# Linear attention and a routed expert layer on one core: the attention's matmuls in fewer array shapes, with a bank for the logits

## The chip, the cores and the metric

One core of a Trainium2 chip runs the whole program. The time is device time in microseconds (us) of one execution; the figure compared is the median of several runs. Lower is better. The engines: PE is TensorE (PEld its weight loads), DVE is VectorE, ACT is ScalarE, POOL is GpSimd, SP issues most DMAs.

## The reference

A gated linear attention over 4 batches and 8 heads, 768 positions, 48 channels, and then an expert layer in which every token goes to one of 8 experts with a capacity of 384 tokens:

```python
for t in range(S):
    state = alpha[:, :, t, :, None] * state + np.einsum('bhd,bhe->bhde', k[:, :, t], v[:, :, t])
    y[:, :, t] = np.einsum('bhd,bhde->bhe', q[:, :, t], state)
...
x = attn_out.transpose(0, 2, 1, 3).reshape(B * S, H * D)     # 3072 x 384
logits = x @ w_gate                                          # 3072 x 8
order = np.argsort(-logits.flatten())                        # best pairs first, each expert at most N // E tokens
...
out[mask] = np.maximum(x[mask] @ w1[e], 0.0) @ w2[e]         # for each expert e
```

## The kernel before

The attention is cut into chunks of C = 128 positions, 6 for each batch. A step `s` (24 in all) works on four chunks `u` of one pair of heads `p`; four steps with the same `g` make a group of 512 tokens. Channels lie on partitions, the two heads of a pair at 0 and at 64 (48 channels each, padded to 64). A step does this:

- DMA loads `al`, `rk`, `rq`, `rv` (alpha, k, q, v).
- VectorE scans alpha backwards into `te` (L349: the product of alpha from a position to the end of its chunk) and forwards into `tp` (L353). `zb`, two banks of PSUM, holds the additive term of the scans; its entries at the starts of chunks are set by a small copy (L364) and a reciprocal (L369). POOL multiplies: `kh` = k times `te`, `qh` = q times `tp` (L361; VectorE in step 0).
- `ends` (L357, VectorE) puts each chunk's whole decay, once for each head with zeros for the other (`hm` is a mask of ones and zeros), into `m`, one of six small buffers in `zb`.
- TensorE transposes `kh` (L378) and ScalarE copies it to `kn`. Scores `kh` x `qh` (L390), 64 rows by 128 columns of the array for each head; ScalarE copies them to `sm` and POOL masks them.
- State products `kn` x `rv` (L406, `st`), 48 columns for each head, outputs at partitions 0 and 64. VectorE (L420; ScalarE for a first chunk, L417) carries them from chunk to chunk into `ts`. `carried` (L426) multiplies the four states with `m` into `sb`, 128 columns wide, the off-diagonal blocks zero.
- The output `yb`: `inter` (L434, the carried product) multiplies `sb`, 128 columns, with `qh`; `intra` (L441, the masked product) adds `sm` x `rv`, 48 columns for each head. ScalarE copies it to `yt` (L444).
- TensorE turns `yt` into rows (L378 again), ScalarE copies them to `xg` (L454), and after four steps they are stored in `x_dram` (L458).
- Logits (L469): for the step two before, in the same operation as the state products and in the same bank, `yt` is the weight (128 columns) and 8 columns of `wg` are the data, a part for each pair `p`. After the fourth, VectorE sums the four parts (L479) into `L`.

The order on each engine is written out beforehand by a list scheduler, `Plan.order`: each operation has a cost, buffers (`Kind`, with a given number of tiles), operations that it must follow, a rank, and on TensorE a `mode`, the array's shape. Among those that can start within `SLACK` of the first it takes the highest rank, with a bonus of `SAME` for the mode that stands; a change of mode is costed at `SWITCH`. Each engine then runs its list in that order and waits where data is not there. The framework keeps two engines apart that touch the same PSUM bank. `choice(b)` puts the first part of the routing (the best expert of each token, the first comparison and counts) for 12, 8 and 4 token blocks into the same list, ranked low.

After the attention, the tokens of an expert are found by a search (L604 comparisons on VectorE, L651 counts on TensorE, L660), and gathered; then come two matrix products for each expert (L868, L888).

Of the kernel before, what the change touches and what calls it, by code (L numbers as in the profile page):

```python
# [8 lines left out]
F32 = mybir.dt.float32  # L9
# [9 lines left out]
AF = mybir.ActivationFunctionType  # L19
OP = mybir.AluOpType  # L20
# [18 lines left out]
class Plan:  # L39
# [10 lines left out]
    def add(self, eng, cost, fn, r=(), w=(), lat=None, port=False, mode=None):  # L50
        n = len(self.ops)
        before, bufs = set(), []
        for x in r:
            if x in self.writer:
                before.add(self.writer[x])
            self.readers.setdefault(x, []).append(n)
        for x in w:
            before.update(self.readers.pop(x, ()))
            if x in self.writer:
                before.add(self.writer[x])  # L60
            self.writer[x] = n
# [83 lines left out]


HOP = {"PE": 0.3, "DVE": 0.15, "ACT": 0.2, "POOL": 0.2, "SP": 2.2}
SLACK, SAME, SWITCH = 0.1, 3.0, 0.15


@with_exitstack
def gla_moe_kernel(ctx, tc, q, k, v, alpha, w_gate, w1, w2, out):
    nc = tc.nc
    C = 128
    NC = 6
    H = 8
    HP = H // 2
# [4 lines left out]
    D = Dm // H  # L162
    E = w_gate.shape[1]
# [3 lines left out]
    consts = ctx.enter_context(tc.tile_pool(name="consts", bufs=1))  # L167
# [4 lines left out]
    ident = consts.tile([128, 128], F32)  # L172
    make_identity(nc, ident)
    L = consts.tile([128, NU, E], F32)
    wg = consts.tile([128, HP, 32], F32)

    T = 128
    BITS = (7, 7, 6, 6, 6)
# [88 lines left out]
    NS = NG * HP  # L267
    X = mybir.AxisListType.X
# [6 lines left out]
    def ring(n, shape, name, ordered=True):  # L275
        return Kind([ap_.tile(shape, F32, name=f"{name}{i}") for i in range(n)], ordered)
# [3 lines left out]
    TE, TP = ring(3, [128, 4 * C], "te"), ring(2, [128, 4 * C], "tp")  # L280
# [17 lines left out]

    nc.vector.memset(zb, 0.0)
    for h in range(2):  # L300
        nc.vector.memset(hm[64 * h:64 * h + 64, h:h + 1], 1.0)
    nc.vector.memset(ST.tiles[0], 0.0)
    nc.gpsimd.memset(wg, 0.0)
    for t in SB.tiles + TS:
        nc.gpsimd.memset(t, 0.0)
# [27 lines left out]
    def step(s):  # L333
        g, p = divmod(s, HP)
        al, rk, rq, rv = load(s)
        te, tp, kh, qh, kn, sm, m, sb, yt = (pl.buf(x) for x in (TE, TP, KH, QH, KN, SM, MR, SB, YT))
        xt, sc, yb, st = (pl.buf(x) for x in (XT, SC, YB, ST))
        parts = 2 if s < 2 else 1
        w = 4 * C // parts
        for j in range(parts):  # L340
            lo, hi = j * w, (j + 1) * w
            us = slice(lo // C, hi // C)
            n = us.stop - us.start

            def each_u(b):
                return [(b, u) for u in range(us.start, us.stop)]

            def scan_e(lo=lo, hi=hi):
                nc.vector.tensor_tensor_scan(te.t[:, lo:hi][:, ::-1], al.t[:, lo + 1:hi + 1][:, ::-1],  # L349
                                             zb[:, lo + 1:hi + 1][:, ::-1], 1.0, op0=OP.mult, op1=OP.add)  # L350

            def scan_p(lo=lo, hi=hi):
                nc.vector.tensor_tensor_scan(tp.t[:, lo:hi], al.t[:, lo:hi], zb[:, lo:hi], 1.0,  # L353
                                             op0=OP.mult, op1=OP.add)

            def ends(us=us, lo=lo, hi=hi, n=n):
                nc.vector.tensor_tensor(m.t[:, us], te.t[:, lo:hi:C][:, :, None].to_broadcast([128, n, 2]),  # L357
                                        hm[:, None, :].to_broadcast([128, n, 2]), op=OP.mult)

            def mul(eng, out_, x, f, us=us, lo=lo, hi=hi):  # L360
                eng.tensor_tensor(out_.t[:, us].rearrange("p u c -> p (u c)"), x.t[:, lo:hi], f.t[:, lo:hi], op=OP.mult)  # L361

            if j == 0:
                add(V, 0.1, lambda: nc.vector.tensor_copy(zb[:, C:4 * C + 1:C], al.t[:, 4 * C + 1:4 * C + 5]),  # L364
                    r=[al], w=["Z"])
            add(V, 0.06 + 0.285 * n, scan_e, r=[al], w=each_u(te) + ["Z"])
            ek, ck, en = (V, 0.08 + 0.15 * n, nc.vector) if s == 0 else (G_, 0.06 + 0.28 * n, nc.gpsimd)
            add(ek, ck, lambda f=mul: f(en, kh, rk, te), r=each_u(te) + [rk], w=each_u(kh), port=True)
            add(V, 0.17, lambda lo=lo, hi=hi: nc.vector.reciprocal(zb[:, lo:hi:C], te.t[:, lo:hi:C]),  # L369
                r=each_u(te), w=["Z"])  # L370
            add(V, 0.06 + 0.285 * n, scan_p, r=[al, "Z"], w=each_u(tp))
# [24 lines left out]

        us_st = [u for u in every if chunk(s, u) < NC - 1]

        back = ys.pop(s - 2, None)

        def state():
            if back:
                logit(st, *back)
            for u in us_st:
                for h in range(2):
                    nc.tensor.matmul(st.t[64 * h:64 * h + D, u, :D], kn.t[:, u, 64 * h:64 * h + D], rv.t[:, u, h],  # L406
                                     start=True, stop=True)
# [16 lines left out]
        def carried():  # L424
            t = ts[:, 4:0:-1] if g % 2 else ts[:, 0:4]
            nc.vector.tensor_tensor(sb.t[:, :, :, :D], t[:, :, None, :].to_broadcast([128, 4, 2, D]),  # L426
                                    m.t[:, :, :, None].to_broadcast([128, 4, 2, D]), op=OP.mult)
        add(V, 0.5, carried, r=[("T", p), m], w=[sb])

        us_y = [u for u in every if chunk(s, u)]  # L430

        def inter():
            for u in us_y:
                nc.tensor.matmul(yb.t[:, u], sb.t[:, u].rearrange("p h d -> p (h d)"), qh.t[:, u],  # L434
                                 start=(u == us_y[0]), stop=False, skip_group_check=True)
# [8 lines left out]
        add(A_, 0.6, lambda: nc.scalar.activation(yt.t, yb.t, AF.Copy), r=[yb], w=[yt])  # L444

        if p == 0:
            grp["xg"] = pl.buf(XG)
        xg = grp["xg"]
        ys[s] = s, yt

        def rows():
            x3 = pl.buf(XT)
# [7 lines left out]
                    r=[(xg, i) for i in range(HP)])  # L460
        return rows

    grp, ys = {}, {}
    wg_ = [("wg", 0), ("wg", 1)]

    def logit(st, s, yt):
        g, p = divmod(s, HP)
        for u in range(4):
            nc.tensor.matmul(st.t[:, p, D + E * u:D + E * u + E], yt.t[:, u], wg[:, p, :E], start=True, stop=True)  # L469

    def logit_reads(back):
        return [back[1]] + wg_ if back else []

    def gather_logits(st, back):
        if not back:
            return
        g, p = divmod(back[0], HP)
        if p == HP - 1:
            add(V, 0.25, lambda: nc.vector.tensor_reduce(  # L479
                L[:, 4 * g:4 * g + 4].rearrange("p u e -> p (u e)"),  # L480
                st.t[:, :, D:D + 4 * E].rearrange("p b x -> p x b"), axis=X, op=OP.add), r=[st], w=[("L", g)])

    def last_logits(s):
        st, back = pl.buf(ST), ys.pop(s)
        add(P_, 0.6, lambda: logit(st, *back), r=logit_reads(back), w=[st], mode=128)
        gather_logits(st, back)
    consts_ = ['init%d' % i for i in range(40)]
    BATCHES = ((0, 3), (3, 5), (5, 6))

# [489 lines left out]
```

## Time and profile before

| | |
|---|---|
| median of 3 runs | 453.09 us (452.11 to 453.66) |
| the profiled execution | 454.3 us, span 452.6 us |
| attention, first VectorE work to the last logits | 8.1 to 147.1 us of the span |
| routing of the first expert | about 147 to 174 us |
| experts | about 174 us to the end |
| mean granted clock of TensorE | 0.934 |

The profile has a page (busy time of each engine; the span in 40 slices, a digit for each) and views of the trace: groups of instructions, what waited for what, the chain that ended last, the order of time, stretches. Times are from the span's start. A row such as `72.08 1.16 PE L434 MATMUL y<-qh,sb 128*128 128x128 f32 x8` reads: start, length until the last of them ends, engine, line, operation, output<-inputs, rows*columns of the array, the data streamed, and how many records; an fp32 matmul leaves two records, a transpose one. Lengths of neighbouring matmul groups overlap, since matmuls are pipelined; from start to start is the better measure.

### The profile page before, as it was taken

Reading aid. Unit: us, or ns where it says so; the run is one execution under the profiler, and the core shown is the slowest. Engines: PE = TensorE matmul, PEld = TensorE weight load, DVE = VectorE, ACT = ScalarE, POOL = GpSimd, SP = SyncE. Lnnn points to the kernel's source line nnn. Section 1 sums busy time; section 2 is a strip of 40 time slices with the busy share of each in tenths; the row PEclk is TensorE's granted clock in tenths of the full one; section 3 lists DMA queues with packets and bytes.
Section 4 is the critical chain, followed back from the end, with each engine's and each line's share of the span. In section 5 each row is a group of like instructions: output and inputs, shape, how many; then the busy total and the mean of one; then the engine's idle time right before and its main releaser. Section 6 shows DMA issues by size and latency. Waiting matters only on the chain.

```text
span 452.6 us, 10133 instructions
## 1 busy us (share of the span) xinstructions
PE 411.9 (91%) x3976; PEld 371.5 (82%) x3976; DVE 276.4 (61%) x816; ACT 213.0 (47%) x353; POOL 187.2 (41%) x196
## 2 busy tenths in 40 slices
PE   3899999999999338998999999999999999999992
PEld 1688888888888235788898998888988999999992
DVE  6998777799772576267686685865866641312110
ACT  1445544554542006336728456373645666575311
POOL 6686666666750005104415255064064062440202
PEclk8899999999999655589999999989999999999997
DMA  8967886753010127979999999999795999996101
GB/s 288 375 193 244 283 275 187 246 177 106 19 71 2 70 92 169 228 133 318 190 246 262 215 292 269 224 282 206 215 271 137 269 272 313 252 238 121 54 0 52
DMA packets 44080, 88.85 MB, mean 196 GB/s; under 512 B 3840, under 2 KB 18176, under 8 KB 44032
## 3 DMA queue, kind: packets, MB, share of 16 engines
q0 software_dynamic: 11776, 34.61, 36.0%
q1 hardware_dynamic: 32256, 53.60, 35.6%
q8 instruction: 31, 0.51, 0.4%
q14 instruction: 17, 0.14, 0.1%
HBM read 53.59 MB, written 9.44 MB: 139 GB/s over the span
## 4 chain that ended last, share of the span: by engine, by line
PE 67%; DVE 12%; issue 9%; DMA 6%; ACT 2%; POOL 2%; POOLq 0%; SPq 0%; DVEq 0%; ACTq 0%
PE h L868 17%; PE y L888 16%; PE rt L651 6%; PE st L469 5%; PE s L390 5%; PE y L441 4%; PE y L434 4%; PE xt L378 4%; DMA w1r<-in_moe_w_dram 3%; DVE cmp L604 2%; PE st L406 2%; DMA w1lo<-w1r 2%; DVE tp L353 1%; DVE te L349 1%; PE xt L852 1%
## 5 line engine op out<-in xcount | busy, mean ns | idle before, releaser
L873 DVE SCALAR_TENSOR_TENSOR hl<-h,hh 128x384 fp32r<-128x384 f32 x64 | 35.4, 554 | 63.9 <-ACT hh L872 61.8
L872 ACT ACTIVATE hh<-h 128x384 fp32r<-128x384 f32 x64 | 31.0, 486 | 79.0 <-PE h L868 69.2
L888 PE MATMUL y<-w2hi,hh 128*128 128x384 f32 x192 | 66.9, 348 | 0.8 <-ACT hh L872 0.8
L888 PE MATMUL y<-w2hi,hl 128*128 128x384 f32 x192 | 66.2, 346 | 0.0
L888 PE MATMUL y<-w2lo,hh 128*128 128x384 f32 x192 | 66.0, 344 | 0.0
L899 POOL DMA_INDIRECT out_dram<-yt,idx x24 | 29.0, 1208 | 58.6 <-ACT yt L892 53.7
L799 POOL DMA_INDIRECT xr<-x_dram,idx x24 | 30.6, 1275 | 51.9 <-DVE val L730 30.2
L868 PE MATMUL h<-xh,w1lo 128*128 128x384 f32 x192 | 48.8, 355 | 1.0 <-DMA w1lo<-w1r 1.0
L827 ACT ACTIVATE w1hi<-w1r 128x768 fp32r<-128x768 f32 x32 | 26.9, 839 | 48.1 <-DVE val L720 21.9
L868 PE MATMUL h<-xl,w1hi 128*128 128x384 f32 x192 | 48.5, 354 | 0.0
L868 PE MATMUL h<-xh,w1hi 128*128 128x384 f32 x192 | 48.3, 356 | 0.0
L832 POOL DMA_DIRECT2D w1lo<-w1r x16 | 22.0, 1378 | 52.8 <-ACT w1lo L828 30.4
L361 POOL TENSOR_TENSOR kh<-rk,te 128x512 f32<-128x512 f32 (+1 forms) x24 | 29.4, 1225 | 34.8 <-DVE z L369 27.3
L651 PEld LDWEIGHTS <-cmp 128*128 128x128 bf16 x816 | 30.5, 118 | 15.3 <-DVE cmp L604 12.4
L651 PE MATMUL rt<-o,cmp 128*128 128x8 bf16 x816 | 33.1, 175 | 8.6 <-DVE cmp L604 8.6
L888 PEld LDWEIGHTS y<-w2hi,hh 128*128 128x128 f32 x192 | 36.6, 190 | 1.9 <-ACT hh L872 1.1
L868 PEld LDWEIGHTS h<-xh,w1lo 128*128 128x128 f32 x192 | 35.6, 197 | 2.0 <-DMA w1lo<-w1r 1.6
L868 PEld LDWEIGHTS h<-xl,w1hi 128*128 128x128 f32 x192 | 35.4, 197 | 2.0 <-issue 1.8
L888 PEld LDWEIGHTS y<-w2lo,hh 128*128 128x128 f32 x192 | 36.5, 190 | 0.3 <-DMA w2lo<-w2r 0.3
L888 PEld LDWEIGHTS y<-w2hi,hl 128*128 128x128 f32 x192 | 36.5, 190 | 0.1
L868 PEld LDWEIGHTS h<-xh,w1hi 128*128 128x128 f32 x192 | 35.7, 198 | 0.8 <-ACT xh L855 0.7
L832 POOL DMA_DIRECT2D w2lo<-w2r x16 | 15.7, 980 | 47.3 <-ACT w2lo L828 46.7
(164 smaller groups left out, 847.0 us busy)
## 6 DMA issues: line engine op xcount, KB each, us to landing
w1r<-in_moe_w_dram SPq DMA_DIRECT2D x16, 768.0 KB, 7.5
w2r<-in_moe_w_dram SPq DMA_DIRECT2D x16, 768.0 KB, 7.9
w1lo<-w1r POOLq DMA_DIRECT2D x16, 768.0 KB
w2lo<-w2r POOLq DMA_DIRECT2D x16, 768.0 KB
al<-in_alpha_dram SPq DMA_DIRECT2D x24, 260.0 KB, 4.2
rk<-in_k_dram SPq DMA_DIRECT2D x24, 256.0 KB, 3.6
rq<-in_q_dram SPq DMA_DIRECT2D x24, 256.0 KB, 4.2
rv<-in_v_dram SPq DMA_DIRECT2D x24, 192.0 KB, 2.5
```

What stands on the lines that cost most here:

```text
L361: eng.tensor_tensor(out_.t[:, us].rearrange("p u c -> p (u c)"), x.t[:, lo:hi], f.t[:, lo:hi], op=OP.mult)
L390: nc.tensor.matmul(sc.t[:, h, u], kh.t[hs, u], qh.t[hs, u], start=True, stop=True)
L469: nc.tensor.matmul(st.t[:, p, D + E * u:D + E * u + E], yt.t[:, u], wg[:, p, :E], start=True, stop=True)
L651: nc.tensor.matmul(cnt, cmp[:, j // U, :, j % U], o[:, j], start=(j == 0), stop=(j == NU - 1))
L799: last_gather[0] = nc.gpsimd.indirect_dma_start(out=XR[i][:, b], out_offset=None, in_=x_dram, in_offset=bass.IndirectOffsetOnAxis(ap=IDX[i ...
L827: nc.scalar.activation(hi[ix_], raw_[ix_], AF.Copy)
L832: nc.gpsimd.dma_start(lo.bitcast(F32), raw_, accum_op=OP.add, max_dma_last_dim=8192)
L868: nc.tensor.matmul(o, a[:, d], x[:, d], start=(n == 0), stop=(n == 3 * DB - 1))
L872: nc.scalar.activation(hh, o, AF.Relu)
L873: nc.vector.scalar_tensor_tensor(hl, o, 0.0, hh, op0=OP.max, op1=OP.subtract)
L888: F2[i, q] = nc.tensor.matmul(Y[b], a[:, bs], w, start=(q == 0 and n == 0), stop=(q == FB - 1 and n == 2))
L899: st_ = nc.gpsimd.indirect_dma_start(out=out, out_offset=bass.IndirectOffsetOnAxis(ap=IDX[i][:, b:b + 1], axis=0), in_=yt, in_offset=None)
```

## The change

- The carried product runs as two matmuls of 64 columns for each chunk, one for each head, with outputs at partitions 0 and 64. It is given the planner's mode 48, that of the masked product and the states.
- The logits are computed in the step itself, as soon as `yt` is there: `wg`, now 64 columns wide with zeros behind the 8, is the weight, and `yt` streams, 128 columns; two chunks for each half of the array. All four steps of a group add up in a bank `LG` of their own. After the fourth, ScalarE copies them (`lt`), TensorE turns them into rows and VectorE copies the 8 columns into `L`. The reduction L479 is gone, and so are the logits after the last step.
- `zb` shrinks to one bank, which makes room for `LG`. The mask `hm` and the factors `m8` move into unused columns of the bank of the states, `ST`; a step's factors are held with its states.
- Since `zb` no longer has a column behind the last position, the last column of `te` is copied by ScalarE, and the scan starts one position earlier from a value read from `al`.
- `choice(b)` enters the list two steps earlier. The planner's constants change.

```diff
-SLACK, SAME, SWITCH = 0.1, 3.0, 0.15
+SLACK, SAME, SWITCH = 0.02, 6.0, 0.17
...
-    wg = consts.tile([128, HP, 32], F32)
+    wg = consts.tile([128, HP, 64], F32)
...
-    SC, YB, ST = (Kind([bank(n, [128, x, 4, C] if x > 1 else [128, 4, C])])
-                  for n, x in (("s", 2), ("y", 1), ("st", 1)))
-    zb = bank("z", [128, 8 * C])
-    MR = Kind([zb[:, 5 * C + 8 * i:5 * C + 8 * i + 8].rearrange("p (u c) -> p u c", c=2) for i in range(6)])
-    hm = zb[:, 6 * C:6 * C + 2]
+    SC, YB, ST, LG = (Kind([bank(n, [128, x, 4, C] if x > 1 else [128, 4, C])])
+                      for n, x in (("s", 2), ("y", 1), ("st", 1), ("lg", 1)))
+    zb = bank("z", [128, 4 * C])
+    hm = ST.tiles[0][:, 0, D:D + 2]
+    LT = ring(2, [128, 2, C], "lt")
...
             def scan_e(lo=lo, hi=hi):
-                nc.vector.tensor_tensor_scan(te.t[:, lo:hi][:, ::-1], al.t[:, lo + 1:hi + 1][:, ::-1],
-                                             zb[:, lo + 1:hi + 1][:, ::-1], 1.0, op0=OP.mult, op1=OP.add)
+                top = min(hi, 4 * C - 1)
+                nc.vector.tensor_tensor_scan(te.t[:, lo:top][:, ::-1], al.t[:, lo + 1:top + 1][:, ::-1],
+                                             zb[:, lo + 1:top + 1][:, ::-1],
+                                             al.t[:, 4 * C + 4:4 * C + 5] if hi == 4 * C else 1.0,
+                                             op0=OP.mult, op1=OP.add)
...
-            def ends(us=us, lo=lo, hi=hi, n=n):
-                nc.vector.tensor_tensor(m.t[:, us], te.t[:, lo:hi:C][:, :, None].to_broadcast([128, n, 2]),
-                                        hm[:, None, :].to_broadcast([128, n, 2]), op=OP.mult)
...
+            add(A_, 0.2, lambda: nc.scalar.activation(te.t[:, 4 * C - 1:], al.t[:, 4 * C + 4:4 * C + 5], AF.Copy),
+                r=[al], w=[(te, 3, "last")])
...
-            add(V, 0.16, ends, r=each_u(te), w=[m])
...
-        back = ys.pop(s - 2, None)
-
         def state():
-            if back:
-                logit(st, *back)
             for u in us_st:
...
-        add(P_, 0.045 * len(us_st) + (0.6 if back else 0.0), state, r=[kn, rv] + logit_reads(back), w=[st], mode=48)
-        gather_logits(st, back)
+        add(P_, 0.045 * len(us_st), state, r=[kn, rv], w=[st], mode=48)
+        m8 = ST.tiles[0][:, 1, D:D + 8].rearrange("p (u c) -> p u c", c=2)
+        add(V, 0.17, lambda: nc.vector.tensor_tensor(
+            m8, te.t[:, 0::C][:, :, None].to_broadcast([128, 4, 2]), hm[:, None, :].to_broadcast([128, 4, 2]),
+            op=OP.mult), r=[(te, u) for u in every], w=[(st, "m")])
...
-                                    m.t[:, :, :, None].to_broadcast([128, 4, 2, D]), op=OP.mult)
-        add(V, 0.5, carried, r=[("T", p), m], w=[sb])
+                                    m8[:, :, :, None].to_broadcast([128, 4, 2, D]), op=OP.mult)
+        add(V, 0.55, carried, r=[("T", p), (st, "m")], w=[sb])
...
             for u in us_y:
-                nc.tensor.matmul(yb.t[:, u], sb.t[:, u].rearrange("p h d -> p (h d)"), qh.t[:, u],
-                                 start=(u == us_y[0]), stop=False, skip_group_check=True)
-        add(P_, 0.225 * len(us_y), inter, r=[sb] + [(qh, u) for u in every], w=[yb], mode=128)
+                for h in range(2):
+                    nc.tensor.matmul(yb.t[64 * h:64 * h + 64, u], sb.t[:, u, h], qh.t[:, u],
+                                     start=(u == us_y[0]), stop=False, skip_group_check=True)
+        add(P_, 0.225 * len(us_y), inter, r=[sb] + [(qh, u) for u in every], w=[yb], mode=48)
...
+        def logit():
+            for b in range(2):
+                for h in range(2):
+                    nc.tensor.matmul(lg.t[64 * h:64 * h + 64, b], wg[:, p], yt.t[:, 2 * b + h], start=(p == 0 and b == 0),
+                                     stop=(p == HP - 1 and b == 1), skip_group_check=True)
+        add(P_, 0.43, logit, r=[yt, ("wg", 0), ("wg", 1)], w=[lg], mode=48)
+        if p == HP - 1:
+            lt, x2 = pl.buf(LT), pl.buf(XT)
+
+            def turn_logits():
+                for b in range(2):
+                    nc.tensor.transpose(x2.t[:, b], lt.t[:, b], ident)
+            add(A_, 0.4, lambda: nc.scalar.activation(lt.t, lg.t[:, :2], AF.Copy), r=[lg], w=[lt])
+            add(P_, 0.22, turn_logits, r=[lt], w=[x2], mode=128)
+            add(V, 0.2, lambda: nc.vector.tensor_copy(
+                L[:, 4 * g:4 * g + 4].rearrange("p (b h) e -> p b h e", h=2),
+                x2.t[:, :2].rearrange("p b (h e) -> p b h e", h=2)[:, :, :, :E]), r=[x2], w=[("L", g)])
...
-    def logit(st, s, yt):
-        g, p = divmod(s, HP)
-        for u in range(4):
-            nc.tensor.matmul(st.t[:, p, D + E * u:D + E * u + E], yt.t[:, u], wg[:, p, :E], start=True, stop=True)
...
-            add(V, 0.25, lambda: nc.vector.tensor_reduce(
-                L[:, 4 * g:4 * g + 4].rearrange("p u e -> p (u e)"),
-                st.t[:, :, D:D + 4 * E].rearrange("p b x -> p x b"), axis=X, op=OP.add), r=[st], w=[("L", g)])
...
-        if s == NS - 1:
-            last_logits(s - 1)
-            last_logits(s)
         for b, (_, y) in enumerate(BATCHES):
-            if y * HP + 1 == (s if s < NS - 1 else s + 2):
+            if y * HP - 1 == s:
```

More of the change, by code (lines that the diff above doesn't have):

```diff
@@ L292, in gla_moe_kernel @@
     XT = Kind([bank("xt", [128, 4, C], psx) for _ in range(2)], ordered=False)
-    SC, YB, ST = (Kind([bank(n, [128, x, 4, C] if x > 1 else [128, 4, C])])
-                  for n, x in (("s", 2), ("y", 1), ("st", 1)))
-    zb = bank("z", [128, 8 * C])
-    MR = Kind([zb[:, 5 * C + 8 * i:5 * C + 8 * i + 8].rearrange("p (u c) -> p u c", c=2) for i in range(6)])
-    hm = zb[:, 6 * C:6 * C + 2]
+    SC, YB, ST, LG = (Kind([bank(n, [128, x, 4, C] if x > 1 else [128, 4, C])])
[3 more added lines that the diff above has]
+    LT = ring(2, [128, 2, C], "lt")
     nc.vector.memset(zb, 0.0)
+    nc.vector.memset(LG.tiles[0], 0.0)
+    nc.vector.memset(ST.tiles[0], 0.0)
     for h in range(2):
         nc.vector.memset(hm[64 * h:64 * h + 64, h:h + 1], 1.0)
-    nc.vector.memset(ST.tiles[0], 0.0)
     nc.gpsimd.memset(wg, 0.0)
@@ L335, in step @@
         al, rk, rq, rv = load(s)
-        te, tp, kh, qh, kn, sm, m, sb, yt = (pl.buf(x) for x in (TE, TP, KH, QH, KN, SM, MR, SB, YT))
+        te, tp, kh, qh, kn, sm, sb, yt = (pl.buf(x) for x in (TE, TP, KH, QH, KN, SM, SB, YT))
         xt, sc, yb, st = (pl.buf(x) for x in (XT, SC, YB, ST))
@@ L363, in step @@
             if j == 0:
-                add(V, 0.1, lambda: nc.vector.tensor_copy(zb[:, C:4 * C + 1:C], al.t[:, 4 * C + 1:4 * C + 5]),
+                add(V, 0.165, lambda: nc.vector.tensor_copy(zb[:, C:4 * C:C], al.t[:, 4 * C + 1:4 * C + 4]),
                     r=[al], w=["Z"])
-            add(V, 0.06 + 0.285 * n, scan_e, r=[al], w=each_u(te) + ["Z"])
+                add(A_, 0.2, lambda: nc.scalar.activation(te.t[:, 4 * C - 1:], al.t[:, 4 * C + 4:4 * C + 5], AF.Copy),
+                    r=[al], w=[(te, 3, "last")])
+            add(V, 0.08 + 0.285 * n, scan_e, r=[al], w=each_u(te) + ["Z"])
             ek, ck, en = (V, 0.08 + 0.15 * n, nc.vector) if s == 0 else (G_, 0.06 + 0.28 * n, nc.gpsimd)
-            add(ek, ck, lambda f=mul: f(en, kh, rk, te), r=each_u(te) + [rk], w=each_u(kh), port=True)
+            add(ek, ck, lambda f=mul: f(en, kh, rk, te), r=each_u(te) + [rk, (te, 3, "last")], w=each_u(kh), port=True)
             add(V, 0.17, lambda lo=lo, hi=hi: nc.vector.reciprocal(zb[:, lo:hi:C], te.t[:, lo:hi:C]),
                 r=each_u(te), w=["Z"])
-            add(V, 0.06 + 0.285 * n, scan_p, r=[al, "Z"], w=each_u(tp))
+            add(V, 0.08 + 0.285 * n, scan_p, r=[al, "Z"], w=each_u(tp))
             add(ek, ck, lambda f=mul: f(en, qh, rq, tp), r=each_u(tp) + [rq], w=each_u(qh), port=True)
-            add(V, 0.16, ends, r=each_u(te), w=[m])
         def turn(dst, src):
@@ L446, in step @@
         if p == 0:
-            grp["xg"] = pl.buf(XG)
-        xg = grp["xg"]
-        ys[s] = s, yt
+            grp["xg"], grp["lg"] = pl.buf(XG), pl.buf(LG)
+        xg, lg = grp["xg"], grp["lg"]
+        def logit():
[14 more added lines that the diff above has]
+                x2.t[:, :2].rearrange("p b (h e) -> p b h e", h=2)[:, :, :, :E]), r=[x2], w=[("L", g)])
         def rows():
@@ L461, in step @@
         return rows
-    grp, ys = {}, {}
-    wg_ = [("wg", 0), ("wg", 1)]
-    def logit(st, s, yt):
-        g, p = divmod(s, HP)
-        for u in range(4):
[L469 to L479, printed above, removed]
-                L[:, 4 * g:4 * g + 4].rearrange("p u e -> p (u e)"),
-                st.t[:, :, D:D + 4 * E].rearrange("p b x -> p x b"), axis=X, op=OP.add), r=[st], w=[("L", g)])
[L483 to L486, printed above, removed]
+    grp = {}
     consts_ = ['init%d' % i for i in range(40)]
```

## The prediction

> **What bounds the kernel now.** I read the page first (span, engine shares, clock), then the table of stretches, then the order of time of one step in the middle of the attention, then the waits, and last the handover to the routing. The page:
>
> ```profile
> span 452.6 us, 10133 instructions
> PE 411.9 (91%) x3976; PEld 371.5 (82%) x3976; DVE 276.4 (61%) x816; ACT 213.0 (47%) x353; POOL 187.2 (41%) x196
> PEclk8899999999999655589999999989999999999997
> ```
>
> The profiled execution took 454.3 us for this span of 452.6 us; the median of the runs is 453.09 us (452.11 to 453.66), 1.2 us less. I add up against 454.3 and take the 1.2 us off at the end. The clock row is low in slices 14 to 18, the routing after the attention; in the attention TensorE has its full clock. The stretch from VectorE's first work to the end of its last product with the carried states:
>
> ```profile
> 8.00:142.30 134.30, 128.66 (x1604) 112.93 (x1604) 108.85 (x252) 63.80 (x109) 83.84 (x73) 0.98 0.59 193
> ```
>
> TensorE is busy in 128.7 of 134.3 us (after the length stand the busy us of TensorE's matmuls and weight loads, VectorE, ScalarE and GpSimd, called POOL, then clock and DMA). Nothing but that stretch is edited, and the rest starts after it, so a microsecond taken from it is a microsecond of the whole. One step of 24, on TensorE, in order of time (start, length, group):
>
> ```profile
> 65.32 1.16 PE L390 MATMUL s<-qh,kh 64*128 64x128 f32 x16
> 66.41 1.16 PE L434 MATMUL y<-qh,sb 128*128 128x128 f32 x8
> 67.50 1.08 PE L441 MATMUL y<-sm,rv 128*48 128x128 f32 x16
> 68.51 1.06 PE L469 MATMUL st<-wg,yt 128*128 128x8 f32 x8
> 69.50 0.47 PE L406 MATMUL st<-rv,kn 128*48 128x48 f32 x12
> 69.90 0.66 PE L378 MATMUL xt<-ident,kh 128*128 128x128 f32 x4
> 70.39 0.60 PE L378 MATMUL xt<-ident,yt 128*128 128x128 f32 x4
> 70.92 1.16 PE L390 MATMUL s<-qh,kh 64*128 64x128 f32 x16
> ```
>
> From start to start: scores 1.09, carried product (L434) 1.09, masked product (L441) 1.01, logits (L469) 0.99, states (L406) 0.40, the two transposes 1.02; together 5.60 us, with no idle time. An fp32 matmul is two records. The masked product has 16 records where the carried one has 8 in hardly more time: its two heads, 48 columns each in the two halves of the array, run side by side. The four middle groups take 69.90 - 66.41 = 3.49 us and alternate between 128 and 48 columns.
>
> **What a record and a change of shape cost.** From the chain, where lengths run from start to start:
>
> ```profile
> 44.72 0.86 PE y L434 x6
> 80.78 0.49 PE st L406 x16
> 105.02 0.59 PE xt L378 x4
> ```
>
> Three carried calls take 0.86 and four 1.09, so one call is 0.23 and the rest, about 0.18, is the change of shape into and out of the group. Four transposes take 0.59 and eight 1.02: 0.108 a record, 0.15 for the change. If a pair of records of the masked product takes 0.108 too, its 8 pairs are 0.86 and the change is 0.15. States: 16 records 0.49, 12 records 0.40, so a pair is about 0.045 and the change 0.13. Once the planner put states and masked product, both of 48 columns, side by side:
>
> ```profile
> 140.29 0.47 PE L406 MATMUL st<-rv,kn 128*48 128x48 f32 x12
> 140.59 1.04 PE L441 MATMUL y<-sm,rv 128*48 128x128 f32 x16
> 141.57 0.43 PE L527 MATMUL xt<-o,cmp 128*128 128x8 bf16 x8
> ```
>
> The two take 1.28 us here against 0.40 + 1.01 = 1.41: one change less is worth 0.13 us.
>
> **The change part by part.**
>
> *Carried product as pairs of 64 columns, in one shape with its neighbours.* Four calls become eight in four pairs: 8 pairs of records at 0.108 are 0.86, as 4 x 0.23 = 0.91 before. The pairing itself gains almost nothing; what goes is the 0.18 of changing shape. No row has 64 columns. The nearest are these (weight loads of 48 and 128 columns, mean ns after the comma) with the paired rows of L441:
>
> ```profile
> L441 PEld LDWEIGHTS y<-sm,rv 128*48 128x48 f32 x384 | 19.8, 123 | 2.8 <-issue 0.3 <-POOL kh L361 0.2
> L434 PEld LDWEIGHTS y<-qh,sb 128*128 128x128 f32 x160 | 19.7, 191 | 3.7 <-DVE sb L426 0.8 <-ACT yt L444 0.5
> L417 ACT ACTIVATE ts<-st 128x48 f32<-128x48 f32 x16 | 3.4, 210 | 14.5 <-DVE ts L420 6.6 <-PE st L406 3.1 <-PE xt L378 2.7
> ```
>
> 68 ns more for 80 more columns is 0.85 ns a column, so a load of 64 columns takes 14 ns longer than one of 48, and about 54 ns of the array's time. A pair of records lasts 108 ns, so I take the load as hidden, as that of 48 columns is. Bounds: nothing, or the whole 54 ns in each pair of records (a rival below).
>
> *Logits the other way round.* Before: four calls with 128 columns of weights and 8 columns of data, 0.99 us with its changes of shape. After: wg's 64 columns are the weights and yt streams; four calls in two pairs, 4 pairs of records, 0.43 us.
>
> *Sum of the four groups*, where they stand together as one block: 0.86 + 0.86 + 0.43 + 0.27 (6 pairs of states) + 0.15 for one change = 2.57 instead of 3.49. With three carried calls 0.86 + 1.01 + 0.99 + 0.41 = 3.27 becomes 0.65 + 0.86 + 0.43 + 0.27 + 0.15 = 2.36. Either way 0.9 us a step. For how many steps? The first two are paced by others:
>
> ```profile
> 20.52 1.28 POOL qh L361
> 21.84 1.16 PE s L390 x16
> ```
>
> Only from step 2 on, at 21.84 us, is the chain on TensorE. 22 steps x 0.9 = 19.8 us off.
>
> *Logits back into rows, six times.* A ScalarE copy of 256 columns, two transposes and a VectorE copy replace a VectorE reduction. TensorE pays 2 x 0.108 = 0.22 if they stand beside other transposes, 0.37 alone: 1.3 to 2.2, I take 1.8 us on. ScalarE (64 of 134 us busy) and VectorE (a copy for a reduction) have it covered by other steps' work, except the last, below.
>
> *te's last column from ScalarE.* 26 one-column activations, at most the 0.21 us of the 48-column row: 5.5 us on ScalarE, hidden by its 70 idle us. They stand ahead of POOL's kh, which waits for them; queued behind one sm copy of about 1 us they would cost POOL that, and POOL has 50 us idle. I take nothing; without that cover it is 0.2 us for each of 24 steps, 5 us. The scan now reads its start value from memory: no row shows it. Between 0 and 0.1 us each (the 48-column ts update, which reads a factor so, is 0.1 us over a small copy), I take 0, at the most 2.4 us of VectorE.
>
> *Factors beside the states.* The 26 small products become 24, on the same engine, for the same 0.17 us. They now write the bank that TensorE's states use, so states of the next step wait until the carried product's operand sb has been made. Behind that wait stand, in TensorE's queue, the logits and transposes. The wait is covered: see VectorE's step.
>
> ```profile
> 65.31 0.55 DVE L426 TENSOR_TENSOR sb<-ts,z 128x384 f32<-128x384 f32 x1
> 65.98 1.21 DVE L349 TENSOR_TENSOR_SCAN te<-al,z 128x512 f32<-128x512 f32 x1
> 67.22 0.19 DVE L369 RECIPROCAL z<-te 128x4 f32<-128x4 f32 x1
> 67.52 1.22 DVE L353 TENSOR_TENSOR_SCAN tp<-al,z 128x512 f32<-128x512 f32 x1
> 68.77 0.17 DVE L364 COPY z<-al 128x4 f32<-128x4 f32 x1
> 68.97 0.17 DVE L357 TENSOR_TENSOR z<-te,z 128x8 f32<-128x8 f32 x1
> 70.02 0.86 DVE L420 SCALAR_TENSOR_TENSOR ts<-ts,te,st 128x48 f32<-128x48 f32 x3 [0.88 <-PE st L406]
> 70.92 0.55 DVE L426 TENSOR_TENSOR sb<-ts,z 128x384 f32<-128x384 f32 x1
> ```
>
> sb is made at 65.86 and the next states come at 69.50: 3.6 us of cover, 2.7 after the step has shrunk.
>
> *VectorE, the engine that is late next.* Its step of 5.61 us has 0.88 us of waiting, so 4.7 us of work and gaps, and TensorE's new step is 4.7. Over the stretch:
>
> ```profile
> DVE ts L420 <- PE st L406: 14.7, 13, 2.5
> DVE ts L420 <- ACT ts L417: 3.0, 7, 1.4
> ```
>
> With 0.8 more for the reduction these are 18.5 us of waits in 134.3: VectorE needs 115.8 us without any, TensorE now 134.3 - 19.8 + 1.8 = 116.3. Two engines so evenly loaded, with rings of two to four buffers between, will not both run without a gap. Bounds for what that costs: 0 (all waits vanish) to 6 (a third of them stays); I take 2.5, nearer to none because the planner can let routing work of low rank, which now becomes ready two steps earlier, slide into the end, where VectorE waits anyway.
>
> *The planner's constants* (a change of shape priced at 0.17, 6 us of preference for the same shape) let the four groups stand together; they have no price beyond the order.
>
> *The end.*
>
> ```profile
> 145.39 0.60 ACT L444 ACTIVATE yt<-y 128x512 f32<-128x512 f32 x1 [3.11 <-PE y L441]
> 146.04 0.97 PEld L469 LDWEIGHTS st<-wg,yt 128*128 128x128 f32 x8 [0.35 <-ACT yt L444]
> 146.95 0.64 PE L378 MATMUL xt<-ident,yt 128*128 128x128 f32 x4
> 147.14 0.29 DVE L479 TENSOR_REDUCE L<-st 128x32 f32<-128x128 f32 x1 [4.80 <-PE st L469]
> 148.14 0.38 SPq L458 DMA_DIRECT2D x_dram<-xg  x1
> 149.93 0.17 PE L658 MATMUL rt<-g,one 128*128 128x8 bf16 x1 [0.33 <-DVE g L535]
> 151.80 0.17 DVE L660 TENSOR_REDUCE k<-rt 128x1 f32<-128x8 f32 x1 [1.92 <-DMA x_dram<-xg]
> ```
>
> The search (k, 151.80) waits for the store of the last rows, not for the logits, which were through at 150.1. The logits' new way (copy under 0.5, transposes about 0.4, three handovers) is some 1 us longer and fits into these 1.7 us; if it did not, it would cost the excess. The store's way gets shorter, since the logits ahead of the last transposes take 0.5 instead of 0.9: 0.4 us off.
>
> **Sum:** -19.8 + 1.8 + 2.5 - 0.4 = -15.9, so 438.4 for an execution like the profiled one and 437.2 us against the median. With 0 to 6 us for the gaps it is 434 to 441.
>
> **The rivals.**
>
> *VectorE becomes the bound.* For it: 115.8 against 116.3 us. Against it: routing work can slide. With a third of its waits left (6.0) and 2.4 us for the scans: -19.8 + 1.8 + 8.4 - 0.4 = -10.0, 443.1 us.
>
> *48 and 64 columns are different shapes,* and changing between them costs the 0.13. Three borders a step: 22 x 0.39 = 8.6 us back, 445.8 us. Nothing in the trace speaks for or against. The Trainium skill, page TensorEngine Tiling (Array Packing), section Tiling Modes, lists tiles of 128, 64 and 32 columns, by which 48 and 64 would be one mode; no run here shows it.
>
> *The weight loads of a pair are exposed:* 54 ns in each of 2 x 3.33 + 4 = 10.7 pairs of records, 0.58 us a step, 12.7 us back: 449.9 us. Against it: a pair of L441 fits the 0.108 us of a transpose's record, with nothing over. The Trainium skill, page TensorE: Matmul & The Clock Gate, section Part 3: Packing small matmuls — row/col tiling, says that weight loads overlap running matmuls only where the row group differs, and in these pairs it is the same. By that rule this rival would be the forecast; the trace of the 48-column pairs disagrees.
>
> *The other side: the states wait for sb.* Place: L406 in TensorE's queue, behind VectorE's sb. If VectorE, now without slack, does a whole preparation (1.21 + 0.19 + 1.22 + 0.17 + 0.17 = 2.96) and a routing comparison of about 1 us before ts and sb, the 2.7 us of cover are exceeded by 1.2 us a step. It decides from 0.9 us a step on, where the gain is gone; at 1.2 it is 22 x 0.3 + 1.4 = 8 us more, 461 us. Against it: ts is made ahead of the next preparation in the rows above.
>
> **How the numbers follow.** Forecast 0.60, VectorE bound 0.20, shape borders 0.06, exposed loads 0.04, the wait for sb 0.10 (0.07 of it slower, 0.03 near no change). A difference under 0.3% (1.4 us) can't be told from none here. Faster 0.90, same 0.03, slower 0.07. The range goes from 434.0 (no gaps at all and the transposes at their cheapest are -18.9, so 434.2) to 446.5, past the shape borders; left out are the last two rivals and a little at the low end, under 0.2.
>
> **What would show it.** L434 with 16 records in about 0.87 us (half the starts coinciding), L469 with 8 in 0.43, no pause between the four groups, 4.7 us from scores to scores; VectorE's wait for the states below 6 us in the attention; the last store's issue near 132 us. Wrong it would be if L434's records came one after the other, if a gap of about 0.1 us stood between the 64- and 48-column groups, or if TensorE waited at L406 or L434 for VectorE by more than 0.3 us a step.

## The result and the profile after

The changed kernel takes 441.01 us (median of 3 runs, 440.52 to 441.85) against 453.09: ratio 0.9739, 95% interval 0.9703 to 0.9775, about 12 us less. Six further runs on another chip, beside eleven of the kernel before, gave 442.62 us and a ratio of 0.9793 (0.9748 to 0.9839), about 9 us less. Some executions of a kernel are slow, over 1.5% above its fastest; ratios leave them out, while a time with its range in brackets is the median of all. The profiled execution took 440.5 us for a span of 438.8 us. The experts' part, which the change leaves alone, took from 269 to 283 us in the profiled executions of this study, with 11 to 38 us of it at half clock; below I therefore compare stretches of the attention and not only whole times.

The page, as shown of the kernel before:

```profile
span 438.8 us, 10527 instructions
PE 398.1 (91%) x4148; PEld 359.3 (82%) x4148; DVE 276.2 (63%) x815; ACT 216.8 (49%) x383; POOL 185.0 (42%) x196
PEclk9999999999998565999998999969999999999997
```

A step on TensorE in which the planner made the full block (start, length, group; L454 is now the logits, L435 the carried product, L442 the masked product, L403 the states):

```profile
62.27 0.66 PE L454 MATMUL lg<-yt,wg 128*64 128x128 f32 x8
62.76 1.04 PE L435 MATMUL y<-qh,sb 128*64 128x128 f32 x16
63.63 1.04 PE L442 MATMUL y<-sm,rv 128*48 128x128 f32 x16
64.50 0.44 PE L403 MATMUL st<-rv,kn 128*48 128x48 f32 x12
64.87 0.66 PE L379 MATMUL xt<-ident,yt 128*128 128x128 f32 x4
65.36 0.60 PE L379 MATMUL xt<-ident,kh 128*128 128x128 f32 x4
65.89 0.66 PE L454 MATMUL lg<-yt,wg 128*64 128x128 f32 x8
66.48 1.16 PE L391 MATMUL s<-qh,kh 64*128 64x128 f32 x16
```

From 62.27 to 64.87 the four groups take 2.60 us; 3.49 before. The logits take 0.49, the carried product 0.87 and the masked one 0.87. Between 64 and 48 columns (62.76 to 63.63 to 64.50) there is no extra time. The next logits (65.89) stand alone between transposes and scores and take 0.59: they bring a change of shape of their own.

The places in the span, before and after, each read from the order of time:

| us of the span | before | after |
|---|---|---|
| first scan | 8.28 | 8.92 |
| scores of step 2 | 21.84 | 24.06 |
| scores of step 23 | 136.78 | 125.15 |
| search begins (k) | 151.80 | 140.34 |
| from step 2 to step 23 | 114.94 | 101.09 |
| from step 2 to the search | 129.96 | 116.28 |

So 13.7 us are won from step 2 on and 2.2 lost before it. The remaining 2.3 of the 13.8 us between the two profiled spans lie behind the search, within the scatter of the experts' part.

The waits of VectorE from its first work to the end of the attention:

```profile
DVE ts L420 <- ACT ts L417: 3.8, 7, 0.9
DVE ts L420 <- PE st L403: 2.9, 3, 1.3
DVE st L407 <- ACT ts L417: 0.6, 1, 0.6
```

They were 18.5 us and are 7.6 (with 0.3 for the copy of the logits). TensorE waited for sb, the feared place, 0.5 us in all, and at the states not at all. It stays the bound: from 24 to 125 us it is busy in 99.5 of 101.0 us, in the kernel before in 114.5 of 114.9 us from 21.8 to 136.7.

The start: the carried and the masked product of step 0 on TensorE, the same of step 1, and VectorE clearing the bank of y.

```profile
17.87 1.55 PE L435 MATMUL y<-qh,sb 128*64 128x128 f32 x12 [0.35 <-DVE sb L426]
19.21 1.73 PE L442 MATMUL y<-sm,rv 128*48 128x128 f32 x16
25.16 0.88 PE L435 MATMUL y<-qh,sb 128*64 128x128 f32 x12
25.86 1.04 PE L442 MATMUL y<-sm,rv 128*48 128x128 f32 x16
6.03 0.48 DVE L313 MEMSET y<- 128x512 f32 x1 [3.20 <-PE y L310]
```

The same records take 1.34 and 1.66 us in step 0, 0.70 and 0.87 in step 1: half the clock. The record of the clock begins with the full share at 20.6 us here (the row of slices shows 9 before it only because nothing was recorded), and gives full clock from 14.4 us in the profile of the kernel before. And VectorE waits 3.2 us for the ten warming matmuls, which take 4.45 us here and 3.67 in the kernel before.

### The profile page after: what moved, and what is told of

It reads as the page before. It is cut to its first block, busy times and chain, and to the rows that moved or that the text cites. A ratio compares the mean times of both kernels' runs of the same rounds, so it can differ in the third digit from the quotient of the medians.

```text
span 438.8 us, 10527 instructions
## 1 busy us (share of the span) xinstructions
PE 398.1 (91%) x4148; PEld 359.3 (82%) x4148; DVE 276.2 (63%) x815; ACT 216.8 (49%) x383; POOL 185.0 (42%) x196
## 4 chain that ended last, share of the span: by engine, by line
PE 68%; DVE 13%; issue 9%; DMA 4%; ACT 2%; POOL 2%; POOLq 0%; SPq 0%; DVEq 0%; ACTq 0%
PE h L860 19%; PE y L880 18%; PE rt L643 6%; PE s L391 4%; PE y L442 4%; PE y L435 4%; PE xt L379 4%; PE lg L454 2%; DMA w1r<-in_moe_w_dram 2%; DMA w1lo<-w1r 2%; DVE cmp L596 2%; DVE tp L357 1%; DVE te L351 1%; PE xt L844 1%; PE st L403 1%
## 5 line engine op out<-in xcount | busy, mean ns | idle before, releaser
L891 POOL DMA_INDIRECT out_dram<-yt,idx x24 | 27.6, 1150 | 60.2 <-ACT yt L884 55.1
L791 POOL DMA_INDIRECT xr<-x_dram,idx x24 | 29.7, 1237 | 50.2 <-DVE val L722 30.3
L361 POOL TENSOR_TENSOR kh<-rk,te 128x512 f32<-128x512 f32 (+1 forms) x24 | 29.5, 1228 | 18.8 <-DVE z L371 11.5
L824 POOL DMA_DIRECT2D w2lo<-w2r x16 | 15.7, 981 | 48.2 <-ACT w2lo L820 47.5
```

Of the source, the lines that this page charges most:

```text
L791: last_gather[0] = nc.gpsimd.indirect_dma_start(out=XR[i][:, b], out_offset=None, in_=x_dram, in_offset=bass.IndirectOffsetOnAxis(ap=IDX[i ...
L824: nc.gpsimd.dma_start(lo.bitcast(F32), raw_, accum_op=OP.add, max_dma_last_dim=8192)
L891: st_ = nc.gpsimd.indirect_dma_start(out=out, out_offset=bass.IndirectOffsetOnAxis(ap=IDX[i][:, b:b + 1], axis=0), in_=yt, in_offset=None)
```

## The experiments

**The logits the old way round, in their own bank.**

```diff
-                    nc.tensor.matmul(lg.t[64 * h:64 * h + 64, b], wg[:, p], yt.t[:, 2 * b + h], ...)
+            for u in range(4):
+                nc.tensor.matmul(lg.t[:, 0, E * u:E * u + E], yt.t[:, u], wg[:, p, :E], ...)   # mode 128
```

> The changed kernel with the logits the old way round (yt as the weights, 8 columns of data, array shape 128), but still in their own bank and added up there, so no transposes at the end of a group. Theory (TensorE is still the bound in most steps): the group goes back from about 0.43 to 0.59 us to 0.9 to 1.0 and brings its changes of shape, 0.4 to 0.5 us in 22 steps, less 6 x 0.3 us for the transposes that fall away: 7 to 9 us over the changed kernel, 448 to 450 us. Rival (VectorE is the bound, TensorE has time to spare): 0 to 3 us over it, 441 to 444 us.

445.8 us (445.4 to 448.4), below the 448 to 450 expected. First scan to search is 137.5 us, 6.1 more than in the changed kernel; the rival, 0 to 3, is out, and the theory was a little too high. One reason is that the planner found the old logits a place between transposes of their own shape:

```profile
52.81 0.66 PE L379 MATMUL xt<-ident,kh 128*128 128x128 f32 x4
53.30 0.96 PE L453 MATMUL lg<-wg,yt 128*128 128x8 f32 x8
54.12 0.63 PE L379 MATMUL xt<-ident,yt 128*128 128x128 f32 x4
```

0.82 us without a change of shape, not 0.99.

**The carried product in 128 columns.**

```diff
-                for h in range(2):
-                    nc.tensor.matmul(yb.t[64 * h:64 * h + 64, u], sb.t[:, u, h], qh.t[:, u], ...)   # mode 48
+                nc.tensor.matmul(yb.t[:, u], sb.t[:, u].rearrange("p h d -> p (h d)"), qh.t[:, u], ...)   # mode 128
```

> The changed kernel with the carried product as before, one matmul of 128 columns for a chunk (planner mode 128). Theory: the pairs gain nothing by themselves, only the changes of shape around them: 0.2 to 0.3 us in 22 steps, 4 to 6.5 us over the changed kernel, 445 to 447.5 us. Rival (VectorE is the bound): 0 to 2 us over it. Second rival (shape changes are what matters, and without this one the block falls apart): 8 us and more.

443.0 us (441.8 to 447.9); first scan to search 136.4 us, 4.9 more. In this stretch, where the clock is granted alike (full from 20.3 us here, from 20.6 in the changed kernel), it is the theory's 4 to 6.5. The whole time came out only 2 us over the first runs of the changed kernel, under the 445 to 447.5 expected; it scatters too much to say more.

**The planner's old constants.**

```diff
-SLACK, SAME, SWITCH = 0.02, 6.0, 0.17
+SLACK, SAME, SWITCH = 0.1, 3.0, 0.15
```

> The changed kernel with the planner's old constants (slack 0.1, bonus 3.0, change of shape 0.15). Theory: the matmuls carry the gain, the order is only a little worse: 0 to 3 us over the changed kernel, 441 to 444 us. Rival (the constants carry it, since they keep groups of one shape together): 6 us or more over it.

439.7 us (438.1 to 441.7), no worse. From step 2 to step 23 it is slower (106.4 us against 101.1, with 100 changes of shape against 77), and it wins that back after step 23: step 2 to search is 117.2 against 116.3. So the constants carry no part of the gain that can be seen here.

**The kernel before with the new constants.**

```diff
-SLACK, SAME, SWITCH = 0.1, 3.0, 0.15
+SLACK, SAME, SWITCH = 0.02, 6.0, 0.17
```

> The kernel before with the new constants alone (0.02, 6.0, 0.17). Theory: within 1.5 us of the kernel before, 451.5 to 454.5 us, since its four groups alternate in shape by their data and not by the planner's choice. Rival (the constants carry the gain): 4 us or more below it.

452.5 us (451.4 to 457.7), ratio to the kernel before 1.000 (0.9955 to 1.0045). As expected.

**The changed kernel again,** the measure for the next three.

> The changed kernel, unaltered, as the measure for the three others of this call: 440 to 442 us if its first runs were typical. The part from the first scan to the search (131.4 us in its first profile) stays within 1 us; the experts' part may differ by 3 us with the clock that is granted there.

442.62 us (440.8 to 445.7); first scan to search 131.5 us, step by step as in the first profile.

**A longer warm-up.**

```diff
-WARM_UP = 10
+WARM_UP = 30
-            nc.tensor.matmul(YB.tiles[0]..., warm[:, :128], warm, start=True, stop=True)
+            nc.tensor.matmul(XT.tiles[1]..., warm[:, :128], warm, start=True, stop=True)
```

> The changed kernel with 30 warming matmuls instead of 10, written to a bank of the transposes, so that VectorE need not wait for them before it clears the bank of y. In the first profile the half clock lasted until 20.6 us, the carried product of step 0 took 1.34 us for 12 records instead of 0.66, and VectorE waited 3.2 us for the warming matmuls. Theory (the late start is part of the missing gain): the scores of step 2 at 21 to 22 us instead of 24.1, 2 to 3 us less in all. Rival (the start is paced by VectorE and POOL, not by TensorE's clock): step 2 moves by less than 0.7 us.

439.09 us (438.1 to 441.0), 3.5 us less than the changed kernel on the same chip; ratio to the kernel before 0.9706 (0.9662 to 0.9750). Scores of step 2 come at 20.13 us, earlier than expected:

```profile
1.40 8.01 PE L310 MATMUL xt<-warm 128*128 128x512 bf16 x30 [1.40 <-POOL warm L169]
14.87 0.88 PE L435 MATMUL y<-qh,sb 128*64 128x128 f32 x12 [0.55 <-DVE sb L426]
15.57 1.04 PE L442 MATMUL y<-sm,rv 128*48 128x128 f32 x16
20.13 1.16 PE L391 MATMUL s<-qh,kh 64*128 64x128 f32 x16
```

The products of step 0 run at full clock, and the first scan begins at 6.66 instead of 8.92 because VectorE no longer waits 3.2 us for the warming matmuls (it waits 1.9 us for POOL before the scan). The edit changes both the number of warming matmuls and the bank, so the share of each is not separated.

**The same in the kernel before.** Its diff is the same two lines.

> The kernel before with the 30 warming matmuls into a bank of the transposes, and nothing else. In the profile of the kernel before the clock happened to be granted from 14.4 us, in that of the changed kernel only from 20.6 us. Theory (the late start belongs to no part of the change, both kernels have it on average): 2 to 4 us under the kernel before, 449 to 451 us, and the difference between the two kernels with the long warm-up is again 12 to 14 us between first scan and search. Rival (the change itself made the start later): at most 1 us under the kernel before.

452.92 us (450.0 to 458.6, and one execution of 573.3 at a granted clock of 0.64) beside 457.74 for the kernel before on that chip; by the ratio, 0.9938 (0.9887 to 0.9989), it is 2.8 us. So the start is not part of the change. The kernel before with the new constants says the same: there too the full clock came only at 20.7 us, and the scores of step 2 at 23.43. With the long warm-up in both, first scan to search is 144.5 and 130.0 us, a difference of 14.5, slightly over what was expected.

**The routing planned around POOL.**

```diff
-            add(V, cost, fn, r=..., w=[(x, b) for x in w])
+            add(V, cost, fn, r=..., w=[(x, b) for x in w], port=not w == ["m"])
-            w=[sm])
+            w=[sm], port=True)
```

> The changed kernel with the routing's small operations on VectorE (all but the first maximum) and POOL's masking declared to the planner as never to overlap each other or POOL's products, the way it already treats kh and qh. In the first profile four such operations took 0.96 to 1.21 us, each ending with a POOL operation, where others of the kind take 0.2. Theory (VectorE, blocked by POOL in the first choice, held TensorE up between steps 12 and 16): the operations take about 0.2 each, and the part from the scores of step 12 to those of step 23 goes from 54.4 to 51 to 53 us. Rival (they would be hidden anyway): within 0.7 us of the changed kernel there. Second rival: the planner has no place for them and they slide to the end, 1 to 3 us later.

440.18 us (438.4 to 441.0), 2.4 less than the changed kernel beside it, but not by the mechanism expected: step 12 to step 23 takes 54.2 us as before (54.4). Most of the operations did become short, two stayed at 1.2. What got shorter is the end, 13.0 us from step 23 to the search instead of 15.2; which operation made it so is not shown. My theory that the first choice held TensorE up in steps 12 to 16 fell with this run.

**The choice joined and late.**

```diff
-    BATCHES = ((0, 3), (3, 5), (5, 6))
+    BATCHES = ((0, 5), (5, 6))
```

> The changed kernel with the first two batches of the choice joined (20 token blocks, ready from step 19). Steps 12 to 19 are then free of it. Theory (the choice on VectorE costs TensorE 3 us there): scores of step 12 to step 19 take 31 to 33 us, as 7 steps of 4.5 to 4.7, instead of 35.8; what is saved comes back in part at the end, where some 5 us of choice have about 4 us of VectorE's waiting to go into: -3 to +1 us in all. Rival (the steps are slow for another reason): no change between steps 12 and 19, and 1 to 4 us more at the end.

439.07 us (436.9 to 443.9), 3.5 less than the changed kernel beside it. Steps 12 to 19 take 34.4 us, not 31 to 33, and steps 12 to 16 the same 19.97 us as in the changed kernel although nothing of the choice is in them. Those steps are long by TensorE's own order, which holds 16 changes of shape in 4 steps where three a step would be 12, and no wait. So the rival was nearly right on those steps, and wrong on the end, which got shorter here too (13.6 us).

**Long warm-up and routing around POOL; and with late choice.**

> The changed kernel with the long warm-up and the routing's small operations planned around POOL. If the two add up (3.8 us earlier search from the one, 2.5 us from the other): search at 134 to 135 us, 436 to 438 us in all. If the early start only fills VectorE sooner: 438 to 440 us.

> As the run before, and the first two batches of the choice joined. If late batches help by having fewer operations: search at 133 to 134.5 us, 435 to 437.5 us. If the joined batch does not fit between POOL's operations near the end: 1 to 3 us over the run before.

The search begins at 134.3 us in the first, as expected, and at 136.5 in the second, 2.2 us over it, as its rival had it; four of the joined batch's small operations still take 1.0 to 1.2 us there, though whether they are the cause is not shown. The times, 441.3 us (434.8 to 445.6) and 443.3 (436.4 to 447.6), scatter too much to rank them. Ratios to the kernel before on that chip: 0.9627 (0.9528 to 0.9726) and 0.9619 (0.9523 to 0.9715), three executions each. Whether they beat the long warm-up alone stays open.

**Both products undone,** the two diffs together.

> The changed kernel with both products undone, logits the old way round in their own bank and carried product of 128 columns; bank, factors, ScalarE's column of te and constants stay. First scan to search: 131.4 us in the changed kernel, 137.5 with the logits undone, 136.4 with the carried product undone, 143.5 in the kernel before. Theory (the two products are the gain and add up): 142 to 144 us there, 450 to 454 us in all. Rival (the other parts have a share of their own): 139 to 141 us.

453.84 us (447.6 to 457.7) beside 457.74, ratio 0.9942 (0.9890 to 0.9993). First scan to search is 142.2 us, in the theory's range, but that stretch holds a start at half clock until 22.9 us. From step 2 to the search, at full clock but for the last 2 us, in which TensorE has hardly any work left, it is 125.6 us, and that is 4.4 less than in the kernel before: the rest of the change has a share, as the rival said. One of its steps:

```profile
54.32 1.16 PE L391 MATMUL s<-qh,kh 64*128 64x128 f32 x16
55.41 1.06 PE L452 MATMUL lg<-wg,yt 128*128 128x8 f32 x8
56.33 0.63 PE L379 MATMUL xt<-ident,yt 128*128 128x128 f32 x4
56.80 0.83 PE L434 MATMUL y<-qh,sb 128*128 128x128 f32 x6
57.47 0.60 PE L379 MATMUL xt<-ident,kh 128*128 128x128 f32 x4
58.00 1.08 PE L441 MATMUL y<-sm,rv 128*48 128x128 f32 x16
58.91 0.44 PE L403 MATMUL st<-rv,kn 128*48 128x48 f32 x12
59.28 1.16 PE L391 MATMUL s<-qh,kh 64*128 64x128 f32 x16
```

With the logits an operation of their own, not tied to the states, the planner puts all groups of 128 columns together: three changes of shape in 4.96 us, where the kernel before has six in 5.4 to 5.6. From step 2 to the search, then:

| kernel | us | less than both undone |
|---|---|---|
| before | 129.96 | -4.4 |
| both undone | 125.61 | |
| logits undone, carried as pairs | 122.49 | 3.1 |
| carried undone, logits swapped | 121.20 | 4.4 |
| changed | 116.28 | 9.3 |

Counted in the order of time from step 2 to step 23, the changes of shape are 120 before, 62 with both undone and 77 in the changed kernel. So the 4.4 us go with fewer changes; which part of the rest (bank, earlier choice, constants together with the bank) brings them was not tested. The 9.3 us of the two products do not: the changed kernel has more changes than the one with both undone. There the matmuls themselves got shorter, the logits above all. From start to start, changes of shape included, the groups on TensorE take between step 2 and step 23:

| us | before | both undone | changed |
|---|---|---|---|
| logits | 20.7 | 18.8 | 11.0 |
| carried product | 19.2 | 17.4 | 15.7 |
| masked product | 21.2 | 19.1 | 19.2 |
| states | 9.1 | 8.4 | 7.4 |
| logits back into rows | none | none | 1.9 |

## Why the prediction was right, and where it was off

Faster was right, and 441.0 lies between 434.0 and 446.5; the likeliest value, 437.2, was 3.8 too low. Of the 15.9 us forecast, 11.5 are there when the search begins; 2.2 are missing at the start, 1.05 in the middle and 1.2 at the end.

- *The four groups as one block, 0.9 us a step.* The sizes were right: 2.60 us for a block forecast at 2.57, logits 0.43 to 0.49, the carried product 0.87 for four pairs of calls, no more than its 0.91 before. The pairs run side by side and their weight loads are hidden: 16 records in 0.87 us. A load of 64 columns takes 137 ns on average, one of 48 columns 125, near the 14 ns of difference forecast. So neither the rival of exposed loads nor that of a border between 48 and 64 columns took place. The Trainium skill's page TensorEngine Tiling (Array Packing), section Tiling Modes, lists tiles of 128, 64 and 32 columns, by which 48 and 64 would be one mode, and the trace agrees: 63.63 - 62.76 and 64.50 - 63.63 are both 0.87. The rule in the Trainium skill, page TensorE: Matmul & The Clock Gate, section Part 3: Packing small matmuls — row/col tiling, that weight loads overlap running matmuls only where the row group differs, does not hold here: the pairs have one row group, and 16 records take 0.87 us.
- *That the groups always stand together* is the step that failed in the middle. The sum allowed three changes a step, 63 in the 21 steps from step 2 to step 23; there are 77. At 0.13 to 0.15 us the 14 more are an estimated 2 us, more than the 1.05 that is missing there. Some logits stand between transposes and scores (0.59), and steps 12 to 15 have 16 changes in all.
- *2.5 us for two engines that are nearly even.* VectorE kept 7.6 us of waits, more than I allowed, but this cost TensorE little: from 24 to 125 us TensorE was idle 1.5 us, and 0.4 us in the like stretch before, so the 2.5 were too much. That makes up for a part of the changes above, which is luck. Forecast for that stretch 21 x 0.9 - 5 x 0.3 - 2.5 = 14.9, measured 13.85.
- *The first two steps* I left out of the sum as unchanged. They came 2.2 us later. The long warm-up in both kernels shows that this is the clock's start and the wait for the warming matmuls, not the change: with it the scores of step 2 come at 20.98 us in the kernel before and at 20.13 in the changed one.
- *The end:* forecast 0.9 for step 23, less 0.3, and 0.4 for the last logits, 1.0 together. From the scores of step 23 to the search it was 15.02 and is 15.19 us. The last store was issued at 136.69 us, where about 132 was forecast. That the logits' longer way hides behind the store was right: its result was through at 139.65 and k still waited 0.75 for the store.

```profile
134.90 0.66 PE L454 MATMUL lg<-yt,wg 128*64 128x128 f32 x8 [0.70 <-ACT yt L445]
135.48 0.66 PE L379 MATMUL xt<-ident,yt 128*128 128x128 f32 x4
139.65 0.17 PE L650 MATMUL rt<-g,one 128*128 128x8 bf16 x1 [0.69 <-DVE g L530]
140.34 0.17 DVE L652 TENSOR_REDUCE k<-rt 128x1 f32<-128x8 f32 x1 [0.75 <-DMA x_dram<-xg]
```

  The 0.4 itself was won from the logits (134.90 to 135.48). What was not won is step 23's share: the last steps are a chain of handovers (states, ts, sb, carried product) and TensorE waits in it. Which of them sets the 15.2 us I did not isolate; planning the routing around POOL shortened it by 2.2. Part of it is only where the order puts step 23's scores: with the old constants the middle is 5.3 us longer and the end 4.4 shorter.
- *The bank, the factors, ScalarE's column* I priced at nothing. The states never waited for sb. The scan with a start value from memory takes 1.28 instead of 1.21 us, within the 0 to 0.1 allowed. But that the logits in a bank of their own are freed from the states, so that the order can do with fewer changes of shape even without the two products, I did not see: 62 instead of 120, and 4.4 us with both products undone. That the bank alone does this was not tested. The sum was still about right, because it counted those changes as part of the block.

## What to carry to other kernels

Where a systolic array's groups alternate in shape, price the changes from the trace (0.13 to 0.15 us each here) and count them. For the carried product, whose work hardly shrank (0.91 to 0.87 us), coming to its neighbours' shape was nearly all of the gain. But look at the work of each group too: the largest item here was the logits, which take 0.43 us with the operands swapped and 0.82 the old way round, without a change of shape in either. An operation that bundles two shapes holds a change that the order cannot remove; splitting it came with half as many changes here. Compare stretches with the same clock, and look at the start, where the first matmuls may run at half speed in one execution and not in another.

## What the hardware showed that I had not expected

Some small VectorE operations of the routing end only with the POOL operation that runs beside them. In the changed kernel:

```profile
88.86 0.96 DVE L501 TENSOR_SCALAR sg<-m 128x12 int32<-128x12 int32 x1
89.86 1.20 DVE L503 TENSOR_TENSOR key<-m,sg 128x12 int32<-128x12 int32 x1
91.09 0.22 DVE L504 TENSOR_TENSOR di<-key,shifts 128x60 int32<-128x60 int32 x1
88.70 1.09 POOL L394 TENSOR_SCALAR_AFFINE_SELECT sm<-sm 128x1024 f32<-128x1024 f32 x1
89.77 1.27 POOL L361 TENSOR_TENSOR qh<-rq,tp 128x512 f32<-128x512 f32 x1
```

sg ends at 89.82 with POOL's masking (89.79), key at 91.06 with its product (91.04); di, with POOL idle, takes 0.22. Planned around POOL, key of the first batch took 0.17, though two others still took 1.2.

The start of the clock varies: with 10 warming matmuls it is full from 14.4 us in one profile, from 15.7 in another and from 19.8 to 22.9 us in the other eight. With 30, in another bank, the whole is 2.8 us shorter in the one kernel and 3.5 in the other.
